# Attention and a gated feed-forward block on one core: the last key tiles of two head pairs in one score chunk

## The chip, the core and the metric

One core of a Trainium2 chip runs the whole program. It has five engines that work side by side and wait for each other through semaphores: TensorE (PE, matrix multiplies, with PEld for its weight loads), VectorE (DVE), ScalarE (ACT), GpSimd (POOL) and SyncE (SP, which here only starts DMAs). Matmul results land in PSUM, everything else lives in SBUF. The metric is the device time of one execution in microseconds, lower is better. The time before is the median of six runs.

## The reference

Causal attention over 8 batches, 8 heads, 576 queries of width 64, with 16 beacon keys and values put ahead of the 576 ordinary ones (592 keys) that every query may see; then a gated feed-forward block over the 4608 tokens:

```python
scores = scale * q @ k_all.T                  # k_all: 16 beacon keys, then k
scores = where(causal, -1e9, scores)          # beacon keys are never masked
a = softmax(scores)
x = (a @ v_all) as (4608, 512)
out = (gelu(x @ w_gate) * (x @ w_val)) @ w_out   # 512 -> 1536 -> 512
```

## The kernel before

**Tiling.** The heads of a batch are worked in four pairs (m = 0 to 3); the two heads of a pair sit in partitions 0 to 63 and 64 to 127 of `qkT`, so that a score matmul uses 64 rows of TensorE and two run side by side. Scores are computed transposed: a tile of up to 128 keys (t = 0 to 4) by the queries that may see it, so the tile of keys t is 576 - `S_LO[t]` queries wide. `CHUNKS` (L28 to L33) packs a pair's five key tiles into four chunks, each at most 512 columns, one PSUM bank per head: chunk 0 is the first 512 columns of tile 0; chunk 1 is the rest of tile 0 with tiles 2 and 4 (480 columns); chunk 2 is tile 1 (464); chunk 3 is tile 3 (208). `scores(b, m, c)` (L243) takes one of two PSUM buffers of the pool `psum_s` (two banks each), writes the chunk for both heads, and has ScalarE write the exponential into `expT` (L276), one SBUF tile per pair with both heads side by side. In batch 0 the causal mask is added in PSUM by small matmuls of `eye` and `neg`; in later batches GpSimd zeroes the diagonal blocks of `expT` afterwards (`masks`, L280), one select per key tile, five per pair.

`attend(b, m)` (L301, called through `av`, L493) multiplies `expT` with the values, 30 matmuls of 65 columns (the 65th gives the sum of the row); `normalize` (L330) divides on VectorE. The result is transposed into `xT_sb`, for pairs 0 and 1 by three DMA transposes on SP (`turn_dma`, L356), for pairs 2 and 3, and all of batch 0, by TensorE (`turn`, L348) with a copy out of PSUM (`put`, L367).

**Feed-forward.** Tokens are worked in nine chunks of 512. For chunk ci, twelve steps of eight matmuls (`gate_val`, `gv_mms`, L379) give gate and value, ScalarE applies the gelu, VectorE multiplies; then 48 output matmuls (`out_mms`, L442) in four groups of twelve, each group followed by a VectorE copy and a store on SP.

**Order.** All instructions stay in program order on each engine (`keep`). In batch b from 1 on (L541 to L602) the 48 output matmuls of chunk b - 1 are dealt out between the attention pieces by `o(n)`; the scores stand in eight bursts of two chunks: `ab(m)` is chunks 0 and 2 of pair m, `cd(m)` chunks 1 and 3. In short:

```python
o(4) ab(0) o(6) cd(0) ahead(2) o(6) ab(1) o(4) av(0) cd(1) ahead(2) o(6) ab(2)
o(4) av(1) cd(2) ahead(2) o(7) ab(3) o(3) av(2) cd(3) o(4) turn(2) o(4) av(3)
```

Then follow the gate and value steps of chunk b. While a burst's two PSUM buffers are still being read by ScalarE, the next burst can't start.

**Loads.** Queries, keys and values are loaded by DMAs that GpSimd starts (`dma`, L117), in program order with the selects. For batches 0 and 1, q and k are transposed by TensorE; from batch 2 on, ten DMA transposes on SP (`transpose_dma`, L230) write `qkT`, in the order q0, k0, q1, k1 to q4, k4 (parts of 128 tokens). The loads of batch 2 are started in batch 1: `qk_loads(2)` is a list of five parts of q, then the beacon keys, then five parts of k; `ahead(n)` starts the next n of them, and what is left goes out at the first gate and value step (L609), ahead of the values of batch 2 and the q and k of batch 3. For later batches all loads go out at that step.

**Batch 0** has no output matmuls to deal out. Its order (L501 to L540) is written out by hand: scores of all four pairs with the transposes of q and k between them, then from L520 on the last pair's chunks with the attends of pairs 0 and 1 between them, turns and copies, the attends of pairs 2 and 3 and the first gate and value matmuls. The attend of pair 1 goes to the one-bank pools `psum_t` and `psum_o`, that of pair 3 to `psum_s`.

Of the kernel before, what the change touches and what calls it, by code (L numbers as in the profile page):

```python
# [7 lines left out]
P = 128  # L8
# [9 lines left out]
NPAIR = H // 2  # L18
# [15 lines left out]
CHUNK_W = [512, 480, 464, 208]  # L34
CHUNK_OFF = [0, 512, 992, 1456]
EXP_W = 1664

EXP_OFF = [0, 992, 576, 1456, 912]
AB, CD = (0, 2), (1, 3)
DV = D + 1  # L40

Q_N = [128, 128, 128, 128, 80]
QK_SCALE = 0.125

FP32 = mybir.dt.float32
BF16 = mybir.dt.bfloat16
ACT = mybir.ActivationFunctionType
# [6 lines left out]
def kernel(  # L54
# [12 lines left out]
    nc = tc.nc  # L67
# [3 lines left out]
    ring = ctx.enter_context(tc.tile_pool(name="ring", bufs=1))  # L71
# [4 lines left out]
    psum_s = ctx.enter_context(tc.tile_pool(name="psum_s", bufs=2, space=bass.MemoryType.PSUM))  # L76
# [11 lines left out]
    wo_sb = const.tile([P, F_TILES, D_MODEL], BF16, name="wo_sb", tag="wo_sb")  # L88
    xT_sb = const.tile([P, NPAIR, N_TOK], BF16, name="xT_sb", tag="xT_sb")

    exp_ring = []
    for r in range(4):
        et = ring.tile([P, 2, EXP_W + P - Q_N[4]], BF16, name=f"expT{r}", tag=f"expT{r}")
        nc.vector.memset(et[:, :, EXP_W:], 0.0)
        exp_ring.append(et)

    NRING = 2
    q_ring, k_ring, v_ring = [], [], []
# [67 lines left out]
    def load_v(b):  # L166
        for load in key_loads(v, beacon_v, v_ring[b % NRING][:, :, :, 0:D], b):
            load()
# [9 lines left out]
    def mm(out_ap, lhsT, rhs, start, stop, **kw):  # L178
        keep(nc.tensor.matmul(out_ap, lhsT, rhs, start=start, stop=stop, **kw))  # L179

    def act(out_ap, in_ap, func, **kw):
        keep(nc.scalar.activation(out_ap, in_ap, func, **kw))  # L182
# [55 lines left out]
                    )  # L238
                )

    exp_of = {}

    def scores(b, m, c):  # L243
        i = b * NPAIR + m
        if c == 0:
            exp_of[i] = exp_ring[i % 4]
        expT = exp_of[i]
        s_ps = psum_s.tile([P, 2, 512], FP32, name="s_ps", tag="s")
        for t, s_lo, w, col in CHUNKS[c]:
            diag = b == 0 and s_lo == S_LO[t]  # L250
            for hi in range(2):
                r = slice(64 * hi, 64 * hi + 64)
                mm(
                    s_ps[:, hi, col : col + w],
                    qkT[r, m, 1, t * P : (t + 1) * P],
                    qkT[r, m, 0, NB + s_lo : NB + s_lo + w],
                    True,
                    not diag,
                    skip_group_check=True,
                )  # L260
            if diag:
                base, n = (NB if t == 0 else 0), DIAG[t]
                for k0, width in ((0, min(n, 64 - base)), (64, n)):
                    for hi in range(2):
                        r = slice(64 * hi, 64 * hi + 64)
                        c0 = 64 + 64 * hi - k0
                        mm(
                            s_ps[:, hi, col : col + width],
                            eye[r, c0 : c0 + P],
                            neg[r, c0 + base : c0 + base + width],  # L270
                            False,
                            k0 == 64,
                            skip_group_check=True,
                        )
        o, w = CHUNK_OFF[c], CHUNK_W[c]
        act(expT[:, :, o : o + w], s_ps[:, :, 0:w], ACT.Exp, scale=QK_SCALE)  # L276
        if b:
            masks(b, m, c)

    def masks(b, m, c):  # L280
        expT = exp_of[b * NPAIR + m]
        for t, s_lo, _, _ in CHUNKS[c]:
            if s_lo != S_LO[t]:
                continue
            n = DIAG[t]
            d = expT[0 : KROWS[t], :, EXP_OFF[t] : EXP_OFF[t] + n]
            keep(
                nc.gpsimd.affine_select(  # L288
                    out=d,
                    in_=d,  # L290
                    pattern=[[0, 2], [1, n]],
                    compare_op=ALU.is_ge,
                    fill=0.0,
                    base=NB if t == 0 else 0,
                    channel_multiplier=-1,
                )
            )
# [3 lines left out]
    def attend(b, m, where="x"):  # L301
        i = b * NPAIR + m
        if where == "ot":
            x_ps = (
                psum_t.tile([P, 512], FP32, name="xt_ps", tag="t"),
                psum_o.tile([P, 512], FP32, name="xo_ps", tag="o"),
            )
            x_of[i] = [(x_ps[hi].rearrange("p (b c) -> p b c", b=1), hi, hi + 1) for hi in range(2)]
        else:
            pool = psum_s if where == "s" else psum_x  # L310
            x = pool.tile([P, 2, 512], FP32, name="x_ps", tag=where)
            x_ps = (x[:, 0, :], x[:, 1, :])
            x_of[i] = [(x, 0, 2)]
        expT, v_sb = exp_of.pop(i), v_ring[b % NRING]
        for j in range(5):
            for hi in range(2):
                for t in range(j + 1):
                    e0 = EXP_OFF[t] + S_LO[j] - S_LO[t]
                    mm(
                        x_ps[hi][:, j * DV : (j + 1) * DV],  # L320
                        expT[0 : KROWS[t], hi, e0 : e0 + P],
                        v_sb[0 : KROWS[t], t, 2 * m + hi, 0:DV],
                        t == 0,
                        t == j,
                        skip_group_check=True,
                    )
# [40 lines left out]
    def put(b, m, by_act=False):  # L367
        y_ps = y_of.pop(b * NPAIR + m)
        out_ap = xT_sb[:, m, b * S : (b + 1) * S]
        if by_act:  # L370
            act(out_ap, y_ps[:, 0:S], ACT.Copy)
        else:
            keep(nc.vector.tensor_copy(out_ap, y_ps[:, 0:S]))  # L373
# [46 lines left out]
    def gate_val(ci, fi, where="s"):  # L420
        gv_mms(ci, fi, *range(K_CHUNKS), where=where, last=True)
# [71 lines left out]
    def av(b, m, where="x"):  # L493
        attend(b, m, where)
        normalize(b, m)

    def c(m, *cs):
        for c_ in cs:
            scores(0, m, c_)

    keep(nc.scalar.preload_act_table_set(SET_EXP))  # L501
    warm(8, psum_x, "x")
# [14 lines left out]
    c(2, *AB)  # L517
    warm(2, psum_x, "x")
    c(2, *CD)
    c(3, 0)  # L520
    av(0, 0)
    c(3, 2)
    av(0, 1, "ot")
    c(3, *CD)
    turn(0, 0)
    put(0, 0)
    av(0, 2)
    turn(0, 1, psum_o, "o")
    put(0, 1, by_act=True)
    av(0, 3, "s")  # L530
    turn(0, 2)
    put(0, 2, by_act=True)
# [8 lines left out]
    for b in range(B):  # L541
        u = [0]

        def o(n):
            out_mms(b - 1, u[0], u[0] + n)
            u[0] += n

        def ab(m):
            for c_ in AB:
                scores(b, m, c_)  # L550

        def cd(m):
            for c_ in CD:
                scores(b, m, c_)

        def ahead(n):
            for _ in range(n):
                if loads:
                    loads.pop(0)()

        loads = qk_loads(b + 1) if b == 1 else []
        if b:
            keep(nc.scalar.preload_act_table_set(SET_EXP))
            o(4)
            ab(0)
            if b == 1:
                transpose_pe(1, 3)
            o(6)
            cd(0)
            ahead(2)  # L570
            o(6)
            ab(1)
            o(4)
            av(b, 0)
            turn_dma(b, 0)
            cd(1)
            ahead(2)
            o(6)
            ab(2)
            o(4)  # L580
            av(b, 1)
            turn_dma(b, 1)
            cd(2)
            ahead(2)
            o(7)
            ab(3)
            o(3)
            av(b, 2)
            cd(3)
            o(4)  # L590
            turn(b, 2)
            put(b, 2)
            o(4)
            av(b, 3)
            keep(nc.scalar.preload_act_table_set(SET_GELU))
            gv_mms(b, 0, 0, 1, 2)
            gv_mms(b, 1, 0)
            turn(b, 3)
            put(b, 3)
            gv_mms(b, 1, 1, 2)  # L600
            gv_mms(b, 0, 3, last=True)
            gv_mms(b, 1, 3, last=True)  # L602
        for fi in range(F_TILES):
            if fi >= 2:
                gate_val(b, fi, "x" if b and fi == 2 else "tx" if fi == F_TILES - 1 and b < B - 1 else "s")
            if b == 0 and 5 <= fi < 11:
                transpose_half(1, (fi - 5) // 2, (fi - 4) % 2)
            if fi == 0:
                ahead(len(loads))  # L609
                if b and b + 1 < B:  # L610
                    load_v(b + 1)
                if b and b + 2 < B:
                    load_qk(b + 2)
                if NPERM <= b + 1 < B:
                    transpose_dma(b + 1)
# [39 lines left out]
```

## Time and profile before

| | us |
|---|---|
| median of six runs | 376.23 (376.04 to 376.97) |
| the profiled execution | 376.26 |
| its span, first to last instruction | 374.6 |
| PE matmuls busy in the span | 365.0 |
| batch 0's attention and first chunk (0 to 48.66) | PE busy 43.16 |
| batch 3's attention (130.32 to 150.54) | 20.22, PE busy 20.12, ACT 14.44, POOL 10.21, DVE 7.40 |
| batch 3's gate and value steps (150.54 to 170.39) | 19.85, PE busy 19.85 |

The last rows are busy times of each engine in stretches of the span. Some lines of the groups (engine, operation, output from input with sizes, count; then busy us, mean ns of one, idle time before them and who ended it):

```profile
L182 ACT ACTIVATE expT<-s_ps 128x1024 bf16<-128x1024 f32 x32 | 32.7, 1023 | 15.1 <-PE s_ps L179 10.9 <-POOL expT L288 4.0
L182 ACT ACTIVATE expT<-s_ps 128x960 bf16<-128x960 f32 x32 | 31.1, 971 | 11.8 <-PE s_ps L179 11.6
L182 ACT ACTIVATE expT<-s_ps 128x928 bf16<-128x928 f32 x32 | 30.0, 938 | 0.4 <-PE s_ps L179 0.4
L182 ACT ACTIVATE expT<-s_ps 128x416 bf16<-128x416 f32 x32 | 16.5, 514 | 0.0
```

These are the four forms of the exponential, one for each chunk, 32 of each in the eight batches. [...]Read the profile with three things in mind: an engine that is busy 40% of the span may still be what the others wait for in one stage; a matmul's recorded duration (379 ns for 512 columns) is longer than its share of the stream; and a wait that several semaphores could have ended is put down to the one that came last.

### The profile page before, as it was taken

How to read it: one execution, taken by the hardware profiler on the slowest of the kernel's cores; microseconds unless marked ns; L12 is line 12 of the kernel's file. 1: busy time of each engine (PE TensorE's matmuls, PEld its weight loads, DVE VectorE, ACT ScalarE, POOL GpSimd, SP SyncE). 2: the span in 40 equal slices, each digit the busy share in tenths (PEclk: the TensorE clock that was granted, in tenths of full speed). 3: DMA queues.
4: the chain of work that ended last, by engine and by line, in shares of the span. 5: the costliest groups of instructions: out<-in, count | busy, mean ns of one | idle time of the engine just before them, and what ended most of it. 6: DMA issues, size and time to landing. Idle time of an engine off the chain costs nothing.

```text
span 374.6 us, 7489 instructions
## 1 busy us (share of the span) xinstructions
PE 365.0 (97%) x3032; PEld 181.3 (48%) x3032; DVE 152.1 (41%) x260; ACT 189.5 (51%) x255; POOL 158.3 (42%) x282
## 2 busy tenths in 40 slices
PE   7799999999999999999999999999999999999996
PEld 3564445544554445444554355445544464444443
DVE  4355544533344425433444235333444244424332
ACT  4853277436753486338733774357534773322210
POOL 8934037874477145832494148624710330000000
PEclk9999999999999999999999999999999999999999
DMA  7999959999889913999299829991590020000102
GB/s 98 171 204 204 194 58 122 124 156 135 78 133 150 140 36 104 145 130 87 64 154 157 73 69 121 131 140 46 114 166 16 33 86 30 0 0 31 56 33 109
DMA packets 149827, 38.34 MB, mean 102 GB/s; under 512 B 136352, under 2 KB 145312, under 8 KB 149792
## 3 DMA queue, kind: packets, MB, share of 16 engines
q0 software_dynamic: 104960, 19.13, 71.6%
q1 hardware_dynamic: 44832, 18.73, 25.8%
q8 instruction: 24, 0.39, 0.4%
q14 instruction: 11, 0.09, 0.1%
HBM read 38.27 MB, written 9.44 MB: 127 GB/s over the span
## 4 chain that ended last, share of the span: by engine, by line
PE 89%; DMA 4%; ACT 2%; issue 2%; SPq 1%; POOL 1%; DVE 0%; POOLq 0%; ACTq 0%
PE gv_ps L179 44%; PE o_ps L179 24%; PE x_ps L179 8%; PE s_ps L179 7%; ACT expT L182 2%; DMA qkT<-q_sb 2%; PE g_ps L179 1%; DMA qk<-in_k_dram 1%; PE v_ps L179 1%; SPq L235 1%; PE t_ps L187 1%; PE y_ps L187 1%; POOL qk L118 0%; DVE y_sb L340 0%; PE xt_ps L179 0%
## 5 line engine op out<-in xcount | busy, mean ns | idle before, releaser
L182 ACT ACTIVATE ge_sb<-gv_ps 128x512 bf16<-128x512 f32 x101 | 59.4, 597 | 134.9 <-PE gv_ps L179 134.9
L182 ACT ACTIVATE expT<-s_ps 128x1024 bf16<-128x1024 f32 (+3 forms) x128 | 103.4, 862 | 27.4 <-PE s_ps L179 22.8
L415 DVE TENSOR_TENSOR hT_sb<-gv_ps,ge_sb 128x512 bf16<-128x512 f32 x101 | 69.1, 690 | 106.2 <-ACT ge_sb L182 103.9
L179 PE MATMUL gv_ps<-xT_sb,wg_sb 128*128 128x512 bf16 x404 | 107.8, 379 | 0.0
L179 PE MATMUL gv_ps<-xT_sb,wv_sb 128*128 128x512 bf16 x404 | 107.7, 379 | 0.0
L179 PE MATMUL o_ps<-wo_sb,hT_sb 128*128 128x512 bf16 (+2 forms) x444 | 107.2, 375 | 0.0
L288 POOL TENSOR_SCALAR_AFFINE_SELECT expT<-expT 128x256 bf16<-128x256 bf16 (+2 forms) x140 | 51.0, 384 | 113.3 <-ACT expT L182 113.3
L179 PEld LDWEIGHTS <-wv_sb 128*128 128x128 bf16 x432 | 42.2, 98 | 51.0
L179 PEld LDWEIGHTS <-wg_sb 128*128 128x128 bf16 x432 | 40.8, 98 | 46.1
L179 PEld LDWEIGHTS <-hT_sb 128*128 128x128 bf16 x444 | 38.0, 98 | 48.8 <-issue 9.9
L434 DVE COPY o_sb<-o_ps 128x512 f32<-128x512 f32 (+2 forms) x37 | 25.0, 675 | 36.9 <-PE o_ps L179 36.8
L179 PE MATMUL s_ps<-qkT 64*128 64x336 bf16 (+5 forms) x384 | 36.4, 282 | 3.3 <-ACT expT L182 1.7
L179 PEld LDWEIGHTS <-expT 128*128 128x128 bf16 (+1 forms) x960 | 33.2, 97 | 7.4 <-issue 0.7
L118 POOL DMA_DIRECT2D v_sb<-in_v_dram x40 | 33.7, 865 | 4.8 <-DMA wg_sb<-in_moe_w_gate_dram 1.6
L118 POOL DMA_DIRECT2D k_sb<-in_k_dram x30 | 25.2, 843 | 22.2 <-DMA q_sb<-in_q_dram 12.4
L179 PE MATMUL x_ps<-v_sb,expT 128*128 128x65 bf16 x930 | 33.5, 193 | 0.6 <-issue 0.6
L338 DVE RECIPROCAL r_sb<-x_ps 128x10 f32<-128x10 f32 x31 | 6.8, 221 | 51.7 <-PE x_ps L179 51.7
L340 DVE TENSOR_TENSOR y_sb<-x_ps,r_sb 128x640 bf16<-128x640 f32 x31 | 25.5, 824 | 1.1
L118 POOL DMA_DIRECT2D q_sb<-in_q_dram x30 | 25.3, 884 | 0.0
L179 PEld LDWEIGHTS <-qkT 64*128 64x128 bf16 x384 | 14.2, 94 | 22.6 <-issue 19.4
L221 DVE COPY qkT<-t_ps 128x576 bf16<-128x576 bf16 x13 | 9.7, 751 | 6.2 <-PE t_ps L187 6.2
L373 DVE COPY xT_sb<-y_ps 128x576 bf16<-128x576 bf16 x16 | 7.3, 456 | 10.8 <-PE y_ps L187 10.8
(50 smaller groups left out, 119.1 us busy)
## 6 DMA issues: line engine op xcount, KB each, us to landing
out_dram<-o_sb SPq DMA_DIRECT2D x35, 256.0 KB, 2.3
v_sb<-in_v_dram POOLq DMA_DIRECT2D x24, 128.0 KB, 6.4
q_sb<-in_q_dram POOLq DMA_DIRECT2D x24, 128.0 KB, 9.3
k_sb<-in_k_dram POOLq DMA_DIRECT2D x18, 128.0 KB, 8.8
wo_sb<-in_moe_w_out_dram POOLq DMA_DIRECT2D x1, 1536.0 KB, 19.0
wg_sb<-in_moe_w_gate_dram POOLq DMA_DIRECT2D x2, 512.0 KB, 11.5
wv_sb<-in_moe_w_val_dram POOLq DMA_DIRECT2D x2, 512.0 KB, 12.9
v_sb<-in_v_dram POOLq DMA_DIRECT2D x8, 112.0 KB, 5.4
```

Of the source, the lines that this page charges most:

```text
L118: keep(nc.gpsimd.dma_start(out=out_ap, in_=in_ap))
L179: keep(nc.tensor.matmul(out_ap, lhsT, rhs, start=start, stop=stop, **kw))
L182: keep(nc.scalar.activation(out_ap, in_ap, func, **kw))
L187: keep(nc.tensor.transpose(out_ap, in_ap, ident[0:n, 0:n]))
L221: keep(nc.vector.tensor_copy(out_ap, in_ap))
L235: nc.sync.dma_start_transpose(out=qkT[:, :, w, c + j * P : c + j * P + n], in_=src[0:n, j, :, :].rearrange("p h d -> p (h d)"),)
L288: nc.gpsimd.affine_select(out=d, in_=d, pattern=[[0, 2], [1, n]], compare_op=ALU.is_ge, fill=0.0, base=NB if t == 0 else 0, channel_multip ...
L338: keep(nc.vector.reciprocal(r, x[:, :, :, D:DV]))
L340: nc.vector.tensor_tensor(out=y_sb[:, :, h0:h1, :].rearrange("p j b d -> p b j d"), in0=x[:, :, :, 0:D], in1=r.to_broadcast([P, h1 - h0, 5 ...
L373: keep(nc.vector.tensor_copy(out_ap, y_ps[:, 0:S]))
L415: nc.vector.tensor_tensor(out=h_of[ci][:, fi, :], in0=gv_of.pop((ci, fi))[1], in1=ge_sb, op=ALU.mult)
L434: keep(nc.vector.tensor_copy(o_sb[:, ti, c0:c1], o_ps))
```

## The change

From batch 1 on, chunk 3 of two pairs shares one PSUM buffer: chunk 3 of pairs 0 and 1 in one, of pairs 2 and 3 in the other. One ScalarE instruction reads both (2 x 208 columns for each head) and writes them to their two places; for that the four `expT` tiles become one tile with the pair as a dimension. `scores` takes a list of (pair, chunk) parts. A batch so has 14 exponentials instead of 16, and they stand in seven bursts of two instead of eight; the output matmuls are dealt out anew, with bursts next to attends. `ahead(2)` stands twice instead of three times. Batch 0 keeps its chunks, but its last part has another order: the attend of pair 0 comes ahead of pair 3's first chunk, that of pair 2 inside pair 3's chunks, and two copies to `xT_sb` change engines. The matmuls and selects are the same in number and size.

```diff
-    exp_ring = []
-    for r in range(4):
-        et = ring.tile([P, 2, EXP_W + P - Q_N[4]], BF16, name=f"expT{r}", tag=f"expT{r}")
-        nc.vector.memset(et[:, :, EXP_W:], 0.0)
-        exp_ring.append(et)
+    exp_ring = ring.tile([P, NPAIR, 2, EXP_W + P - Q_N[4]], BF16, name="expT", tag="expT")
+    nc.vector.memset(exp_ring[:, :, :, EXP_W:], 0.0)
...
-    def scores(b, m, c):
...
+    def scores(b, *parts):
         s_ps = psum_s.tile([P, 2, 512], FP32, name="s_ps", tag="s")
+        c0 = 0
+        for m, c in parts:
+            score_mms(b, m, c, s_ps[:, :, c0 : c0 + CHUNK_W[c]])
+            c0 += CHUNK_W[c]
+        (m, c), n = parts[0], len(parts)
+        o, w = CHUNK_OFF[c], CHUNK_W[c]
+        act(
+            exp_ring[:, m : m + n, :, o : o + w].rearrange("p g h c -> p h g c"),
+            s_ps[:, :, 0 : n * w].rearrange("p h (g c) -> p h g c", g=n),
+            ACT.Exp,
+            scale=QK_SCALE,
+        )
+        if b:
+            for m, c in parts:
+                masks(b, m, c)
...
-    c(3, 0)
     av(0, 0)
-    c(3, 2)
+    c(3, *AB)
     av(0, 1, "ot")
-    c(3, *CD)
+    c(3, 1)
+    av(0, 2)
+    c(3, 3)
     turn(0, 0)
-    put(0, 0)
-    av(0, 2)
     turn(0, 1, psum_o, "o")
-    put(0, 1, by_act=True)
+    put(0, 0, by_act=True)
+    put(0, 1)
     av(0, 3, "s")
...
             o(4)
-            ab(0)
+            scores(b, (0, 0))
+            scores(b, (0, 2))
             if b == 1:
                 transpose_pe(1, 3)
-            o(6)
-            cd(0)
+            o(7)
+            scores(b, (0, 1))
+            scores(b, (0, 3), (1, 3))
             ahead(2)
-            o(6)
-            ab(1)
-            o(4)
+            o(7)
+            scores(b, (1, 0))
+            scores(b, (1, 2))
             av(b, 0)
             turn_dma(b, 0)
-            cd(1)
+            o(4)
+            scores(b, (1, 1))
+            scores(b, (2, 0))
             ahead(2)
-            o(6)
-            ab(2)
-            o(4)
+            o(7)
+            scores(b, (2, 1))
+            scores(b, (2, 2))
             av(b, 1)
             turn_dma(b, 1)
-            cd(2)
-            ahead(2)
-            o(7)
-            ab(3)
-            o(3)
+            o(4)
+            scores(b, (2, 3), (3, 3))
+            scores(b, (3, 0))
+            o(6)
             av(b, 2)
-            cd(3)
+            scores(b, (3, 1))
+            scores(b, (3, 2))
             o(4)
             turn(b, 2)
             put(b, 2)
-            o(4)
+            o(5)
             av(b, 3)
```

More of the change, by code (lines that the diff above doesn't have):

```diff
@@ L239, in transpose_dma, with score_mms @@
                 )
-    exp_of = {}
-    def scores(b, m, c):
[L244 to L247, printed above, removed]
-        s_ps = psum_s.tile([P, 2, 512], FP32, name="s_ps", tag="s")
+    def scores(b, *parts):
+        s_ps = psum_s.tile([P, 2, 512], FP32, name="s_ps", tag="s")
+        c0 = 0
[13 more added lines that the diff above has]
+                masks(b, m, c)
+    def score_mms(b, m, c, s_ps):
         for t, s_lo, w, col in CHUNKS[c]:
@@ L274, in scores @@
                         )
[L275 to L278, printed above, removed]
     def masks(b, m, c):
-        expT = exp_of[b * NPAIR + m]
+        expT = exp_ring[:, m, :, :]
         for t, s_lo, _, _ in CHUNKS[c]:
@@ L313, in attend @@
             x_of[i] = [(x, 0, 2)]
-        expT, v_sb = exp_of.pop(i), v_ring[b % NRING]
+        expT, v_sb = exp_ring[:, m, :, :], v_ring[b % NRING]
         for j in range(5):
@@ L498, in c @@
         for c_ in cs:
-            scores(0, m, c_)
+            scores(0, (m, c_))
     keep(nc.scalar.preload_act_table_set(SET_EXP))
@@ L546, in o @@
             u[0] += n
[L548 to L554, printed above, removed]
         def ahead(n):
```

## The prediction

> **What bounds the kernel.** I read the totals first, then the chain of waits, then the order of time inside one late batch, batch 2 and batch 0.
>
> ```profile
> PE 365.0 (97%) x3032; PEld 181.3 (48%) x3032; DVE 152.1 (41%) x260; ACT 189.5 (51%) x255; POOL 158.3 (42%) x282
> ...
> PE 89%; DMA 4%; ACT 2%; issue 2%; SPq 1%; POOL 1%; DVE 0%; POOLq 0%; ACTq 0%
> ```
>
> TensorE is the bound, at a granted clock of 1.0 in all forty slices. The change removes no matmul, so it can only win in the 374.6 - 365.0 = 9.6 us of idle PE, or in time inside "busy" that is no throughput: a matmul's end is modelled, and its tail covers a gap. Batch 3 shows such gaps (start, duration, instructions, in brackets the idle time before and who ended it):
>
> ```profile
> 130.26 0.59 PE L179 MATMUL s_ps<-qkT 64*128 64x512 bf16 x4
> 130.78 1.47 PE L179 MATMUL o_ps<-wo_sb,hT_sb 128*128 128x512 bf16 x6
> 132.18 0.75 PE L179 MATMUL s_ps<-qkT 64*128 64x64 bf16 x8
> 132.86 1.47 PE L179 MATMUL o_ps<-wo_sb,hT_sb 128*128 128x512 bf16 x6
> ```
>
> A 512-column matmul streams in 0.2155 us (four take 128.44 to 129.30 in that order of time). Six from 130.78 end at 132.07; the scores start at 132.18: 0.11 us lost on entry. The first burst streams 512 + 464 columns, two heads side by side, 976/2400 = 0.407 us (the 2.4 GHz is 512 columns over 0.2155), so it ends at 130.67, and the outputs start at 130.78: 0.11 lost on exit. The second burst has 688 columns, 0.287 us, yet lasts from 132.18 to 132.86: 0.28 us too long beside its switches. The chain says why:
>
> ```profile
> 130.90 0.77 issue
> 131.67 0.95 ACT expT L182
> 132.62 0.04 issue
> 132.66 0.27 PE s_ps L179 x2
> ```
>
> Its last tile (chunk 3) needs the PSUM buffer of chunk 2, whose exponential ends at 132.62. The chain shows this in batches 3 to 7. From 130.78 to the first gate matmul at 148.39 are 17.61 us; the work in it is 44 outputs 9.48, four attends of 0.909 = 3.64, one turn 0.26, 5680 score columns 2.37, sum 15.75. Of the 1.86 left, 0.28 is the stall: 1.58 over 7 bursts, **0.226 us per burst**.
>
> **Here a rule is weighed.** The Trainium skill, "TensorEngine Tiling (Array Packing)", Key Properties, says that changing the tiling mode drains TensorE. Scores are 64*128, all else 128*128, so each burst would pay the full tail twice, 379 - 216 = 163 ns each: 0.33 us. By the rule seven bursts fewer give 2.3 us, by the row 1.58. I take the row.
>
> **The change, part by part.**
>
> *One burst fewer in batches 1 to 7.* Same columns and matmuls: 0.226 each.
>
> *Buffer waits of the new order.* ScalarE's step is its row less 0.1 of tail: the first burst's 1024 and 928 elements take 1.86 together, the 960 and 416 take 1.38, so 0.92, 0.84, 0.866 and 0.41. The joint tile (832) has no row; by the straight line through 416 and 960 it is 0.76, at least 0.69 (832 at 1.2 elements/ns, the slope of that line), at most two old ones (0.82). I take 0.76. New batch 3: outputs 130.78, seven to 132.29; burst 2 at 132.39, first tile to 132.59, the second waits for 132.67: 0.08, where 0.28 stood. Burst 3 at 134.56, with the joint exponential done about 134.6 and wanted at 134.77: no wait, 0.17 to spare. attend 0 then follows its burst directly; its third-tile mask (one POOL select, 406 ns) ends at 135.05, wanted at 135.5. Burst 4 at 136.94, burst 5 at 139.07; its second tile waits for the 1024 exponential of (2,0), 139.36 against 139.27: 0.09. Bursts 6 and 7 find their buffers free. attend 3, at about 147.1, wants the select behind the last exponential at about the same moment; I cost it 0, at most 0.1. GpSimd issues the same 20 selects; ScalarE's two fewer instructions lie in its own idle time.
>
> Gain: batches 3 to 7: 0.226 + 0.28 - 0.08 - 0.09 = 0.336, times 5 = **1.68**. Batches 1 and 2 have no such stall (17.43 us for the same stretch of batch 2): 0.226 - 0.09 = 0.14 each. turn 2 finds y_sb as before (DVE ends it 1.3 us after attend 2, an output group and a burst lie between); the xT copies by SP move with attend 1, 0.2 earlier, and the third lands (2.3 after 145.5) before the gate matmuls want it at 148.2.
>
> *Loads of batch 2 made two fewer ahead.* This is the loss. `ahead(2)` stood three times in batch 1, now twice; q's fifth part and k's beacon rows fall behind batch 1's last select on GpSimd's queue, in front of k's parts.
>
> ```profile
> 62.98 0.70 POOL L118 DMA_DIRECT2D q_sb<-in_q_dram  x1
> 63.67 0.54 POOL L118 DMA_DIRECT2D k_sb<-in_beacon_k_dram  x1
> ...
> 66.20 1.04 POOL L288 TENSOR_SCALAR_AFFINE_SELECT expT<-expT 128x256 bf16<-128x256 bf16 x3 [0.89 <-ACT expT L182]
> 67.19 4.19 POOL L118 DMA_DIRECT2D k_sb<-in_k_dram  x5
> ```
>
> The two cost 0.70 + 0.54 = 1.24 us of POOL; the last select ends 0.28 earlier in the new order (by the same walk, 66.97 against 67.24). So k's loads start 0.96 later. Behind them SP's transposes stand in order: q0, k0 (waits for the load until 71.98), q1, k1 (until 75.06), then one each 1.4 to 1.5 us without a wait to q4 at 82.42. And batch 2's first burst waits for just that one:
>
> ```profile
> 82.42 8.11 DMA qkT<-q_sb
> ...
> 90.67 0.37 PE L179 MATMUL s_ps<-qkT 64*128 64x464 bf16 x2 [0.29 <-DMA qkT<-q_sb]
> ```
>
> The first line is the chain's, the second the order of time on PE. There is no slack here: the 0.96 goes to PE, and batch 1's own 0.14 is swallowed by the same wait. Bounds: 0.5 (a shorter landing; the rows lie between 6.6 and 8.7) and 1.5 (the whole 1.24 and a longer landing). I take 0.96. That the landing is not free time is also the skill's, "Trainium Kernel Development and Optimization", Key Constraints: DMAs of SP, ACT and POOL share the same 16 engines, so a queue of its own doesn't shelter SP's copies from POOL's loads. If only SP's own time counted (1.3 us in the rows), the burst would have been free at 83.8 and the move would cost nothing; the row has 8.11. The end of POOL's stream (92.36 in the trace) moves by about 1.1; batch 2's first values want selects only at 96.
>
> *Batch 0.* ScalarE paces the scores; before, PE waits 0.5 us for a buffer ahead of pair 3's first chunk (17.17), which attend 0 now fills. Walking the new order with the same durations: attend 0 at 16.70, chunks (3,0), (3,2) at 17.72, attend 1 at 18.39, (3,1) at 19.41, attend 2 at 19.88, (3,3) at 20.90, two turns, attend 3 at 21.66 instead of 22.17: 0.5 us. put(0,0) on ScalarE and put(0,1) on VectorE end before the gate matmuls want them. But in attend 3:
>
> ```profile
> 22.17 0.56 PE L179 MATMUL x_ps<-v_sb,expT 128*128 128x65 bf16 x13
> 23.29 0.69 PE L179 MATMUL x_ps<-v_sb,expT 128*128 128x65 bf16 x17 [0.56 <-issue]
> ```
>
> PE stops after 13 of 30 matmuls, though its wait for the last exponential (done 21.95) stands at the sixteenth. Nothing in the trace releases it. It is about the 704th instruction of PE; the page's table of queues has an instruction queue with 24 packets, some 250 of PE's 6066 instructions each, and the DMA engines are 90% busy there, so I suspect that the next block came late. The change keeps attend 3 at the same place in the stream. If the release depends on how far PE has got, it comes about 0.7 earlier as PE is that much earlier before it; if on the clock alone, the gain is 0; if the stop vanishes, 0.5 + 0.7 = 1.2. I take **0.65**, near the first.
>
> *Memsets.* Three fewer at 98 ns on DVE, beside loads: 0.
>
> **Sum.** -0.65 (batch 0) + 0.96 (batch 2's start) - 0.14 - 1.68 = -1.51. The profiled execution took 376.26 us (span 374.6 and 1.66 around it), 0.03 above the median of the runs: 376.26 - 1.5 = **374.7**.
>
> **Rivals.**
> A, as above: 48%, 374.0 to 375.4.
> B, batch 2's copies land no later (POOL's issues overlap, the landings shorten): the 0.96 is gone, 373.8; with the stop in batch 0 gone too, 373.2. For it: landings of 6.6 in batch 3. Against: k0 and k1 were visibly awaited. 17%.
> C, PE gains nothing in batch 0 and the copies come 1.4 later: 1.4 - 0.14 - 1.68 = -0.4, 375.8. For it: the stop looks tied to the crowded DMA engines. 20%.
> D, slower: the joint exponential, whose output now jumps between two pairs, costs far more than its 832 elements. Its buffer is wanted 0.17 after it is done, in burst 3 of seven batches; from 0.93 us on each further nanosecond is PE's, seven times. At 1.5 us it is 7 x 0.57 = 4.0: 378.8; the point from which the change loses is 0.93 + 1.5/7 = 1.15. For it: no row of that shape. Against: rows follow the number of elements closely. Other late selects act the same way, seven times. 15%.
> That the change doesn't do what it says I exclude: the built order has 14 exponentials per batch instead of 16.
>
> **Numbers.** 0.2% is 0.75 us, what a measurement can tell here. A, nearly whole, and B are faster: 0.63. C and A's edge are the same: 0.22. D: 0.15. Range 373.4 to 376.2: A, B and C; beyond it lie D and the best of B.
>
> **What would show it.** Right: scores in seven bursts, each switch still 0.22; between batch 3's first outputs and its gate matmuls 17.3 us; a wait for qkT<-q_sb of 1.2 to 1.5 us in batch 2; the first "issue" stop of attend 3 ended near 22.6. Wrong: a wait for POOL at an attend, a joint exponential over 0.95 us, or batch 2 waiting under 0.5 us.

## The result and the profile after

The changed kernel took 375.33 us (median of 32 runs, 373.17 to 380.02), the kernel before beside it 376.77 (67 runs, 375.55 to 382.28). The ratio, which leaves out one run of the changed kernel in a slower state (380.02 us), is 0.9958, 95% interval 0.9942 to 0.9973: 1.58 us less, between 1.0 and 2.2. The prediction was 1.5 less; its 374.7 us started from a kernel before at 376.23, which ran at 376.77 here.

The profiled execution of the changed kernel is one of its longer ones: 377.53 us, span 375.8, so 1.27 us longer than the profiled execution before. It has to be read stage by stage. Its totals and the engine line of its chain of waits:

```profile
PE 366.5 (98%) x3032; PEld 182.4 (49%) x3032; DVE 152.1 (40%) x257; ACT 188.0 (50%) x241; POOL 159.4 (42%) x282
...
PE 83%; DMA 8%; SPq 2%; POOL 2%; ACT 1%; issue 1%; DVE 0%; ACTq 0%; POOLq 0%
```

DMA has doubled its share of the chain, from 4% to 8%; ScalarE's fell from 2% to 1%. These shares say what the chain runs through, not what was lost: 4% of the span are 15 us, while the two waits for a DMA below are 2.07 and 0.82 us. Where such a wait ends, the chain is followed back through several copies in a row, during most of which PE was busy.

The best ruler is the time from the first gate matmul of one batch to that of the next, taken from the order of time on PE (us; column b starts at the first gate matmul of batch b):

| | start of batch 0's gate | 0 | 1 | 2 | 3 | 4 | 5 | 6 |
|---|---|---|---|---|---|---|---|---|
| before | 24.08 | 43.97 | 40.27 | 40.07 | 40.07 | 40.07 | 40.08 | 40.07 |
| after | 24.71 | 43.77 | 41.92 | 39.72 | 40.66 | 39.73 | 39.72 | 39.72 |

Period b holds the feed-forward steps of batch b and the attention of batch b + 1. Batches 3, 5, 6 and 7 (periods 2 and 4 to 6) take 0.35 less. Against that, batch 2 (period 1) takes 1.65 more and batch 4 (period 3) 0.59. Here is the order of time on PE in batch 5 of the changed kernel (start, duration, instructions):

```profile
212.72 0.59 PE L176 MATMUL s_ps<-qkT 64*128 64x512 bf16 x4
213.24 1.69 PE L176 MATMUL o_ps<-wo_sb,hT_sb 128*128 128x512 bf16 x7
214.86 0.62 PE L176 MATMUL s_ps<-qkT 64*128 64x64 bf16 x10
215.41 1.69 PE L176 MATMUL o_ps<-wo_sb,hT_sb 128*128 128x512 bf16 x7
```

The second burst now has ten matmuls and 480 + 2 x 208 = 896 columns, 0.37 us at 2.4 columns per ns, and lasts from 214.86 to 215.41, 0.55. Before, 688 columns (0.29) took 0.68. So the long wait for chunk 2's exponential is nearly gone. The new exponential is in the groups by shape (count, then busy us, mean ns):

```profile
L179 ACT ACTIVATE expT<-s_ps 128x832 bf16<-128x832 f32 x14 | 12.0, 860 | 4.3 <-PE s_ps L176 4.3
```

From the first outputs at 213.24 to the first gate matmul at 230.51 are 17.27 us, where 17.61 stood in batch 3 before. The two losses are one kind of line:

```profile
92.89 0.37 PE L176 MATMUL s_ps<-qkT 64*128 64x464 bf16 x2 [2.07 <-DMA qkT<-q_sb]
```

This is batch 2's first burst, waiting for SP's transpose of q's last part. It waited 0.29 before. (Batch 4 has the same wait with 0.82; its loads were not touched by the change, and no other profiled execution has it.)

### The profile page after: what moved, and what is told of

It reads as the page before. It is cut to its first block, busy times and chain, and to the rows that moved or that the text cites. A ratio compares the mean times of both kernels' runs of the same rounds, so it can differ in the third digit from the quotient of the medians.

```text
span 375.8 us, 7487 instructions
## 1 busy us (share of the span) xinstructions
PE 366.5 (98%) x3032; PEld 182.4 (49%) x3032; DVE 152.1 (40%) x257; ACT 188.0 (50%) x241; POOL 159.4 (42%) x282
## 4 chain that ended last, share of the span: by engine, by line
PE 83%; DMA 8%; SPq 2%; POOL 2%; ACT 1%; issue 1%; DVE 0%; ACTq 0%; POOLq 0%
PE gv_ps L176 36%; PE o_ps L176 24%; PE s_ps L176 8%; PE x_ps L176 8%; DMA qkT<-q_sb 5%; SPq L232 2%; DMA q_sb<-in_q_dram 2%; PE t_ps L184 2%; DMA k_sb<-in_k_dram 1%; PE g_ps L176 1%; PE v_ps L176 1%; ACT expT L179 1%; POOL v_sb L115 1%; PE y_ps L184 1%; PE w_ps L176 1%
## 5 line engine op out<-in xcount | busy, mean ns | idle before, releaser
L179 ACT ACTIVATE expT<-s_ps 128x960 bf16<-128x960 f32 (+2 forms) x114 | 102.0, 947 | 30.6 <-PE s_ps L176 27.3
L176 PE MATMUL o_ps<-wo_sb,hT_sb 128*128 128x512 bf16 (+2 forms) x444 | 105.9, 374 | 0.0
L292 POOL TENSOR_SCALAR_AFFINE_SELECT expT<-expT 128x256 bf16<-128x256 bf16 (+2 forms) x140 | 52.0, 387 | 114.1 <-ACT expT L179 104.9
L176 PEld LDWEIGHTS <-hT_sb 128*128 128x128 bf16 x444 | 38.8, 98 | 46.1 <-issue 8.6
L176 PEld LDWEIGHTS <-expT 128*128 128x128 bf16 (+1 forms) x960 | 32.2, 97 | 7.7 <-issue 2.6
```

Source lines behind the costliest of these rows:

```text
L292: nc.gpsimd.affine_select(out=d, in_=d, pattern=[[0, 2], [1, n]], compare_op=ALU.is_ge, fill=0.0, base=NB if t == 0 else 0, channel_multip ...
```

## The experiments

### The loads of batch 2

**e1_ahead3**: the changed kernel, with the loads as far ahead as before.

```diff
             scores(b, (3, 0))
+            ahead(2)
             o(6)
```

> The changed kernel with the third pair of loads ahead put back, after the sixth burst of batch 1, so that q's fifth part and k's beacon rows of batch 2 leave before k's five parts again. My theory: the changed kernel lost 0.96 us (0.5 to 1.5) at batch 2's start through this move, its profiled execution even 2.07 of waiting for qkT<-q_sb; with it undone batch 2 waits 0.3 to 0.7 us, and the kernel takes 2.4 us less than before (ratio 0.9935) instead of 1.6 less. Rival B (the copies land no later): the wait and the time stay as in the changed kernel, ratio 0.996.

Ratio to the kernel before 0.9932 (0.9908 to 0.9957), median 375.16 us. Period 1 fell from 41.92 to 40.45, the wait from 2.07 to 0.61; periods 2 to 6 are all 39.72.

```profile
92.39 0.37 PE L176 MATMUL s_ps<-qkT 64*128 64x464 bf16 x2 [0.61 <-DMA qkT<-q_sb]
```

So the loads are the cause of most of batch 2's loss. By the ratios the two fewer ahead cost 0.26% (0.9958 - 0.9932), 1.0 us, with intervals that overlap. The medians, 375.16 against 375.33, hardly differ: of the sixteen runs four lie at 372.5 to 373.0 and the others at 374.8 to 376.8.

**e5_before2**: the reverse, the kernel before with the last `ahead(2)` taken out and nothing else.

```diff
             cd(2)
-            ahead(2)
             o(7)
```

> The kernel before, with only the third pair of loads ahead taken out of batch 1. My theory: this alone brings the loss of the change, batch 2 waits 1.2 to 2.1 us for qkT<-q_sb instead of 0.29, and the kernel takes 0.9 to 1.8 us more, ratio 1.0025 to 1.005; the stretches of batches 3 to 7 stay at periods of 40.07. Rival B: no longer wait, ratio 1.000.

Ratio 1.0021 (0.9997 to 1.0044), so 0.8 us slower, a little less than the 0.9 to 1.8 expected, with an interval that just reaches zero. In its profile the wait was 2.62, and period 1 took 44.18: 3.91 more than before, although the wait grew by 2.33 only. The rest is a slower clock, see the last section.

**e4_early**: the loads a stage earlier, at the last gate step of batch 0.

```diff
-        loads = qk_loads(b + 1) if b == 1 else []
+        loads = qk_loads(2) if b == 0 else []
...
-            if fi == 0:
+            if fi == (F_TILES - 1 if b == 0 else 0):
                 ahead(len(loads))
```

> The changed kernel with all eleven loads of batch 2 started at the end of batch 0's gate and value steps, where GpSimd has nothing queued, instead of four in batch 1 and seven behind it. My theory: SP's transposes for batch 2 then go without a wait for a load, q4's is issued 3 us or more sooner, and batch 2 doesn't wait: 0.29 (the wait before) + 0.96 + 0.14 = 1.4 us better than the changed kernel, ratio to before 0.992. Rival: what delays the copies is the shared DMA engines, not the loads' start; then batch 2 waits 1 to 2 us still, ratio 0.996.

Ratio 0.995 (0.9932 to 0.9968), where 0.992 was expected. Batch 2's wait is gone (period 1: 39.73), but batch 1 pays. The order of time on GpSimd and then that on PE:

```profile
46.84 3.31 POOL L115 DMA_DIRECT2D q_sb<-in_q_dram  x4 [7.21 <-DMA wo_sb<-in_moe_w_out_dram]
...
54.80 1.44 POOL L292 TENSOR_SCALAR_AFFINE_SELECT expT<-expT 128x224 bf16<-128x224 bf16 x4
```

```profile
55.32 1.09 PE L176 MATMUL x_ps<-v_sb,expT 128*128 128x65 bf16 x15 [1.22 <-POOL expT L292]
```

The second load waits 7.21 us for an earlier DMA, that of `wo_sb`, with all of GpSimd's queue behind it. The loads run to 54.8, batch 1's selects come after them, and its first attend waits for those. Period 0 became 47.50 instead of 43.77: the two waits in that attend are 1.46 of the 3.73, and most of the rest is a granted clock of 0.50 from 57.54 to 60.96 (last section).

**e8_best** and **e11_best** (the same kernel twice): one load at batch 0's last gate step, the others spread over batch 1.

```diff
-        loads = qk_loads(b + 1) if b == 1 else []
+        if b == 0:
+            loads = qk_loads(2)
...
             scores(b, (0, 2))
+            ahead(1)
...
             scores(b, (3, 0))
+            ahead(2)
...
-            if fi == 0:
+            if b == 0 and fi == F_TILES - 1:
+                ahead(1)
+            if b and fi == 0:
                 ahead(len(loads))
...
```

> The changed kernel with batch 2's loads spread: one at the end of batch 0 (the second would wait there until the output weights have landed), then one behind the first burst of batch 1 and two each behind the second, fourth and sixth, so that only k's last three parts fall behind its selects. My theory: SP's transposes then run without a wait for a load, q4's is issued about 2 us before that of the kernel before, and batch 2 doesn't wait, while no attend waits for a select: periods of batch 1 and 2 of 43.8 and 39.7, 0.3 to 0.7 us better than with two loads behind the sixth burst alone, ratio to before about 0.992. Rival: two DMA starts more between the selects (0.88 us each) make an attend of batch 1 wait, and its period grows by up to 1 us.

> The version with batch 2's loads spread once more. If the wait in batch 2, and the clock that it costs in some executions, is what separates it from the changed kernel, its ratio to before is 0.990 to 0.993, below that of the changed kernel, and its runs lie closer together.

Ratios 0.9908 (0.9875 to 0.994, six runs) and 0.9921 (0.9889 to 0.9953, nine runs): medians 373.96 and 373.61 us. No wait for `qkT` in batch 2 (period 1: 39.91 and 39.72, against 41.92); batch 1 pays 0.3 (period 0: 44.09 against 43.77). This version is 3.0 to 3.5 us below the kernel before. Beside the changed kernel measured with it (e10_after, 0.996) it is 0.39% or 1.5 us lower; these two intervals just overlap, that of e8_best lies below the changed kernel's first one. The runs do not lie closer together, as e11_best was expected to show: its nine span 372.68 to 376.08, the 22 of e10_after 373.81 to 377.66. So nothing here shows that batch 2's wait is what spreads the runs.

### Batch 0's order

**e2_b0old**: the changed kernel with batch 0's last part in the old order. **e6_b0new**: the kernel before with only that part in the new order.

```diff
+    c(3, 0)
     av(0, 0)
-    c(3, *AB)
+    c(3, 2)
     av(0, 1, "ot")
-    c(3, 1)
-    av(0, 2)
-    c(3, 3)
+    c(3, *CD)
     turn(0, 0)
+    put(0, 0)
+    av(0, 2)
     turn(0, 1, psum_o, "o")
-    put(0, 0, by_act=True)
-    put(0, 1)
+    put(0, 1, by_act=True)
```

(e2_b0old against the changed kernel; e6_b0new is the same edit the other way round on the kernel before.)

> The changed kernel with the old order of the last part of batch 0. My theory: 0.65 us of the gain goes, ratio to before about 0.9977 (1.6 less becomes 0.9 less); from chunk (2,1) to the first gate matmul 8.6 us as before, instead of 7.96. Rival C (batch 0 gained nothing, the release of the stop in attend 3 is on the clock): no difference to the changed kernel, ratio 0.996.

> The kernel before, with only the new order of the last part of batch 0. My theory: from the two warming matmuls ahead of chunk (2,1) to the first gate matmul 8.7 us instead of 9.4, ratio to before 0.998; everything from batch 1 on as before (periods of 40.07). Rival C: nothing, ratio 1.000.

e6_b0new: 0.9979 (0.996 to 0.9997), 0.8 us less. e2_b0old: 0.9997 (0.9977 to 1.0017), so 1.5 us more than the changed kernel, where 0.65 was expected, with a wide interval. The traces are sharper. From the two warming matmuls ahead of pair 2's chunk 1 to the first gate matmul, the old order took 9.39 (before), 9.53 (e2) and 9.24 (e5), the new one 8.74 (after), 8.43 (e1), 9.03 (e3), 8.69 (e4), 8.83 (e6), 8.56 (e7) and 9.11 (e8): means 9.39 and 8.77, a gain of 0.62. In e10_after and e11_best the first of the two warming matmuls is missing from the trace; from the second, with the 0.23 between the two added, both come to about 8.97, which makes the gain 0.57.

### The stop in attend 3

In the changed kernel it is still there, in the order of time on PE:

```profile
22.88 0.53 PE L176 MATMUL x_ps<-v_sb,expT 128*128 128x65 bf16 x12
...
23.91 0.71 PE L176 MATMUL x_ps<-v_sb,expT 128*128 128x65 bf16 x18 [0.50 <-issue]
```

**e7_warm4** puts four matmuls and their weight loads fewer ahead of it on PE:

```diff
-    warm(8, psum_x, "x")
+    warm(4, psum_x, "x")
```

> The changed kernel with four warming matmuls at the start instead of eight: four matmuls and four weight loads fewer in PE's stream, ahead of all data. It asks what the stop in batch 0's attend 3 hangs on. If it stands at a place in the stream of instructions (about the 704th), it moves by eight instructions, so it comes after 16 or 17 of the attend's 30 matmuls instead of 12 or 13. If it hangs on a value (the exponential of chunk (3,3), first read by the 16th) or on a copy, it stays after 12 or 13.

```profile
22.74 0.65 PE L176 MATMUL x_ps<-v_sb,expT 128*128 128x65 bf16 x16
23.70 0.59 PE L176 MATMUL x_ps<-v_sb,expT 128*128 128x65 bf16 x14 [0.31 <-issue]
```

Four matmuls fewer before it, and the stop moves from behind the twelfth to behind the sixteenth: it belongs to a place in PE's instruction stream, not to a semaphore or a moment. The other profiles that have it agree: it stands behind the thirteenth in all three with batch 0's old order and behind the twelfth in the seven others with the new one.

**e9_hold** takes the traffic away from there: most of GpSimd's loads of weights and those of batch 1 move behind one more select, which changes no value and follows pair 3's last chunk.

```diff
-    load_gate_val(4, 8)
-    load_qk6(1, 0, 4)
-    load_kb(1)
-    load_gate_val(8, 12)
-    load_qk6(1, 4, H)
-    load_out_w()
-    load_v(1)
...
     c(3, 3)
+    masks(0, 3, 3)
+    load_gate_val(4, 8)
+    load_qk6(1, 0, 4)
+    load_kb(1)
+    load_gate_val(8, 12)
+    load_qk6(1, 4, H)
+    load_out_w()
+    load_v(1)
```

> The changed kernel with all loads behind the first eight gate and value weight tiles' first half (the weights of steps 4 to 11, q and k of batch 1, output weights, values of batch 1) held on GpSimd until pair 3's last exponential of batch 0 (by one more select on it, which changes no value). It asks whether the stop in attend 3 comes from crowded DMA engines. If so, the engines are far emptier from 18 to 23 us, and the stop of 0.3 to 0.9 us after 12 or 13 of 30 matmuls is gone or under 0.1. If it stays at 0.3 or more, crowding isn't its cause. Later steps wait for their weights, so the whole takes longer; only the stop is asked for.

```profile
24.08 1.26 PE L176 MATMUL x_ps<-v_sb,expT 128*128 128x65 bf16 x30
```

All 30 run through. The busy times between 20 and 24 us (stretch, its length, then PE, PEld, DVE, ACT and POOL with counts, the granted clock, the DMA share, GB/s; the share is the sum of all packets' times over 16 engines' time, so it passes 1 where packets overlap), first of the changed kernel, then of e9_hold:

```profile
20.00:24.00 4.00, 3.50 (x98) 3.12 (x95) 2.75 (x8) 3.19 (x5) 1.89 (x3) 1.00 1.29 206
```

```profile
20.00:24.00 4.00, 4.00 (x107) 3.36 (x104) 2.54 (x7) 3.15 (x5) 0.00 (x0) 1.00 0.19 26
```

206 GB/s with the stop, 26 without it. e9_hold also came to the attend later, at 24.08 instead of 22.88, so a late PE is a rival. It can't be the whole: e1_ahead3 came there at 24.07, with 207 GB/s from 21 to 25 us, and still stopped, for 0.27. Crowding thus rests on one execution, and lateness may shorten the stop. As a whole e9_hold is slower (381.83 us in its single run): its output weights come late, which alone makes PE wait 2.58 us.

### One burst more

**e3_split6**: the changed kernel with the sixth burst cut in two by outputs; columns, exponentials and order stay.

```diff
             scores(b, (2, 3), (3, 3))
+            o(3)
             scores(b, (3, 0))
-            o(6)
+            o(3)
```

> The changed kernel with its sixth burst in two: three of the six output matmuls behind it go between its two tiles. Eight bursts again, the same matmuls, no tile that waits for a buffer. My theory, that each burst costs 0.226 us for its two switches whatever stands in it: in batches 5 to 7 the stretch from the first outputs to the gate matmuls grows from 17.27 to 17.50, in all 7 x 0.226 = 1.6 us, ratio to before about 1.000. By the full drain of the rule: 0.33 each, 2.3 us, ratio 1.002. Rival: the gain of the batches came from the removed buffer stall and the new places of the output matmuls alone; then the stretch stays 17.3, ratio 0.996.

Ratio 1.0015 (0.9993 to 1.0037). The undisturbed periods are 39.93 instead of 39.72: one more entry and exit cost 0.21 us. In seven batches that is 1.5 us; the ratio is 2.1 us above the changed kernel's (0.9958), with an interval that holds the 1.000 of the row and the 1.002 of the rule. Batch 2 waited 2.47 in its profile.

### The changed kernel again

**e10_after** is the changed kernel once more, on the chip of e11_best.

> The changed kernel once more, beside the version with spread loads on the same chip. Ratio to before 0.996; a wait in batch 2 for qkT<-q_sb of 1.2 to 2.8 us, and where it is above about 2.4, a lower granted clock in the matmuls behind it.

Ratio 0.996 (0.9941 to 0.9979), as in the first measurement. Its profile has a wait of 0.98 in batch 2, below the 1.2 to 2.8 expected, where the first had 2.07, with not a line changed: this wait is no constant.

## Why the prediction held, step by step

**The bursts: right.** 0.336 was forecast for each of batches 3 to 7; 0.35 was measured. A burst's price was 0.226 from the row and 0.33 from the rule; e3_split6 says 0.21. The row was the better guide. (Two readings of the prediction are slightly off, without effect: batch 2's stretch before is 90.97 to 108.32, so 17.35 and not 17.43, and PE's instructions are 2 x 3032 = 6064.)

**The buffer waits: right.** The joint exponential was put at 0.76 plus 0.1 of tail, and its mean is 860 ns, so rival D, which needed 1.15, falls. The second burst's wait was put at 0.08; it lasts 0.55 where the same burst, right behind the long wait of batch 2 with both buffers long free, lasts 0.49: 0.06. The fifth burst's was put at 0.09:

```profile
221.58 0.65 PE L176 MATMUL s_ps<-qkT 64*128 64x64 bf16 x8
222.16 1.08 PE L176 MATMUL x_ps<-v_sb,expT 128*128 128x65 bf16 x30
```

It lasts 0.58, its 944 columns 0.39, with 0.11 of a switch 0.50: 0.08 of waiting. attend 3 takes 0.93 us in the chain of the changed kernel where attend 2 takes 0.91 to 0.92: a wait for its select is 0.02 at most.

**Batches 0 and 1: right.** -0.65 was forecast for batch 0; between the marks above it is 0.65 in the two first profiles and 0.57 to 0.62 in the means. Rival C, in which PE gains nothing there, falls. The suspicion behind the number, an instruction block that comes late under crowded DMA engines, is what e7_warm4 and e9_hold support; that PE's progress sets its release also fits: 8.60 us after the warming matmuls before, 7.94 after, 0.66 earlier. Batch 1 gained 0.20 (0.14 forecast).

**Batch 2: the mechanism right, the wait too small in most profiles.** To the step "the 0.96 goes to PE" belonged "a wait for qkT<-q_sb of 1.2 to 1.5 us". Six profiled executions with two loads fewer ahead waited 0.98, 1.47, 2.07, 2.47, 2.62 and 2.83, mean 2.07, so 1.8 more than before. The order of time on GpSimd and on SP's queue in the changed kernel, and the landing of the last copy from its chain:

```profile
68.20 0.54 POOL L115 DMA_DIRECT2D k_sb<-in_beacon_k_dram  x1
68.72 4.20 POOL L115 DMA_DIRECT2D k_sb<-in_k_dram  x5
```

```profile
74.37 1.21 SPq L232 DMA_TRANSPOSE qkT<-k_sb  x1
...
82.62 2.61 SPq L232 DMA_TRANSPOSE qkT<-k_sb  x1
85.32 1.24 SPq L232 DMA_TRANSPOSE qkT<-q_sb  x1
```

```profile
85.32 7.43 DMA qkT<-q_sb
```

All of batch 1 stands 0.43 later here than in the trace of before (first gate matmul 68.48 against 68.05); take that off. k's loads start 1.10 later (0.96 forecast; the last select ended 0.12 earlier, not 0.28). k0's transpose starts 5.65 us after k's loads are begun instead of 4.79, as its load lands later: +0.86. The chain of transposes behind it takes 10.95 from k0 to q4 instead of 10.44: +0.51, as one of them took 2.61. Only q4's own copy is quicker, 7.43 against 8.11: -0.68. The sum is 1.79, and the wait grew by 1.78. The forecast moved the start and kept every later duration as it had been in one execution.

In time, as against waits, the two loads cost 1.0 us by e1_ahead3 and 0.8 by e5_before2, both with wide intervals and both near the 0.96. So whether the profiles drew long waits by chance, or the forecast was too small for most runs as well, is open.

**The sum.** In the two profiled executions, counted from the warming matmuls, it is -0.65 - 0.20 + 1.65 - 5 x 0.35 + 0.94 = -0.01; the 0.94 is batch 4's chance wait (40.66 against 39.72). Without that it is -0.95, and with e10_after's batch 2 (period 1: 40.82, so +0.55) -2.05. The runs say -1.58, between them, and the forecast -1.51. The wait in the runs that were not profiled can't be seen, so how the -1.58 divides is open; that the total came within 0.1 of the forecast is in part luck. The single parts agree with it if they are taken from the kernel before: fewer loads ahead, +0.8 (e5_before2), and batch 0's order, -0.8 (e6_b0new), cancel, which leaves the bursts, -1.75 - 0.20 = -1.95, inside the interval of 1.0 to 2.2 less. Taken from the changed kernel, +1.0 (e1_ahead3) and -1.5 (e2_b0old), the sum is -2.45, just outside it; each part is known to about 1 us only.

Why the profiled execution is 1.27 longer nevertheless: its warming matmuls stand at 15.97 instead of 14.69, 1.28 later, ahead of all that was moved, behind a full clock that came later (last section).

## What to carry to other kernels

When a load is moved that stands at the head of a chain of DMAs without slack, price the chain and not the shift: each landing moved by up to about a microsecond here, and a transfer that comes late moves every issue behind it. A group of short matmuls in another tile shape has a price on entry and exit that can be read from neighbouring rows, and so has an exponential from its element count; both held to some 0.02 us here. Before a gain of 1 us is read from one profile, compare stages between fixed marks, as the first 16 us alone differed by more than that.

## What was not expected

**A wait of over 2 us can cost nearly as much again.** After batch 2's wait in e7_warm4 the order of time on PE shows:

```profile
93.44 0.37 PE L176 MATMUL s_ps<-qkT 64*128 64x464 bf16 x2 [2.83 <-DMA qkT<-q_sb]
93.74 2.28 PE L176 MATMUL o_ps<-wo_sb,hT_sb 128*128 128x512 bf16 x7
```

Seven outputs take 2.28 us instead of 1.69. The granted clock of the stretches around this (columns as above) tells why, first e7_warm4, then the changed kernel:

```profile
91.28:94.70 3.42, 1.26 (x7) 0.61 (x8) 0.00 (x0) 1.24 (x2) 0.54 (x2) 1.00 2.07 153
94.70:98.11 3.41, 3.41 (x18) 1.04 (x17) 0.65 (x1) 1.62 (x3) 0.84 (x3) 0.50 1.05 67
```

```profile
88.49:91.91 3.42, 2.32 (x12) 0.78 (x9) 1.38 (x2) 2.92 (x4) 1.40 (x2) 1.00 1.83 153
91.91:95.32 3.41, 2.44 (x20) 1.03 (x21) 0.00 (x0) 1.00 (x3) 1.02 (x3) 1.00 2.38 151
```

The clock is 0.50 for 3.41 us in the one and stays at 1.00 in the other. Waits of 2.13 (e9_hold), 2.47 (e3_split6), 2.62 (e5_before2) and 2.83 us were followed by such a dip, each of 3.41 us at 0.50; the 2.07 was not. A dip of 3.41 us at half the clock costs PE half of it, some 1.7 us (an estimate). What period 1 lost beyond its wait was 44.39 - 39.72 (a later period) - 2.83 = 1.84 us in e7_warm4, 1.49 in the same way in e5_before2, and 2.19 in e3_split6, of which 0.41 is another wait.

It is not the length of the wait alone that decides. The record of the clock in the traces gives the start of each stretch of full clock and of the dip that ends it: 81.92 us lie between them in e3_split6, e5_before2 and e7_warm4, 78.51 in e9_hold and 51.20 in e4_early. These are 24, 23 and 15 times 3.413, so the clock changes on a grid of that step. The four waits left PE busy for 0.79 to 1.30 of the 3.41 us in one step, and the clock fell in the next. The 2.07 of the changed kernel fell across an edge, at 91.91, with 2.32 and 2.44 us busy in the two steps. The Trainium skill, "TensorE: Matmul & The Clock Gate", Part 1, has the clock fall when an activity window of about 3.4 us, which runs freely, finds PE idle; the step agrees, but a window that was idle for 2.15 of its 3.41 us was enough here. Where the limit lies is open, and busy time is not its whole measure: a step with 1.40 us busy in e9_hold had no dip behind it, one with 1.87 in e4_early, most of it short matmuls of an attend, had.

So the loss of the two loads has a step in it, which the forecast did not have. How often it falls in the unprofiled runs isn't known.

**The clock at the start differs too.** Two lines of the order of time on PE, the same twelve transposes, of the kernel before and of the changed one:

```profile
7.81 0.45 PE L187 MATMUL t_ps<-eye,qk 96*64 96x96 bf16 x12
```

```profile
9.07 0.69 PE L184 MATMUL t_ps<-eye,qk 96*64 96x96 bf16 x12
```

0.69 us instead of 0.45, although the clock column of both stretches says 1.00. The record of the clock in the traces only begins with the first full clock, and the column counts what is ahead of it as full: it begins at 4.32 us in the kernel before and at 13.40 in the changed one, whose transposes take 0.69 up to the group at 12.84 and 0.45 from that at 13.94 on. PE's instructions are the same in both up to there. Over the eleven profiled executions with this opening (all but e7_warm4 and e9_hold) the warming matmuls ahead of pair 2's chunk 1 stand between 14.29 and 17.25, a spread of 3 us and twice the change's gain. It goes with the clock: the three latest, at 17.25, 15.97 and about 15.7, are those whose full clock began latest, at 17.13, 13.40 and 10.66; in the other eight it began by 6.34, and they stand by 14.91. Why it comes late in some executions is open.

**A stop at a fixed place of the instructions.** The stop in attend 3 was 0.3 to 0.9 us in every profile but e9_hold's. The Trainium skill, "Runtime: NRT & Kernel Launch", on instruction fetch, says that instructions come in blocks and that crossing into the next is mostly hidden. That fits the fixed place; if it is this crossing, it was not hidden with the DMA engines at 206 GB/s. The fetch itself no run here shows at that moment.
